# Two PSUM banks as two tiles, splits spread over steps, two activations moved by 128 bytes

## The chip, the cores and the metric

The kernel runs on one core of a Trainium2 chip. The metric is the device time of one execution in microseconds (us); for a kernel that is timed several times it is the median. A profiled execution gives a trace with every instruction; its own time stands beside the span from its first to its last instruction.

## The reference

Packed attention, a multilayer perceptron (MLP) with an ELU-like function, and a second one with a rational function, one after the other on 4608 tokens (8 batches of 576) of 512 features:

```python
p_packed = sm_attn(p, k, v)              # 8 heads x 32 packed rows, softmax over 576 keys
x = sm_attn(q, p_packed, p_packed)       # 576 queries over the 32 packed rows
h = x @ w_in                             # 512 -> 2048
g = np.where(h > 0.0, h, np.exp(np.minimum(h, 0.0)) - 1.0)
x = g @ w_out                            # 2048 -> 512
h = x @ w_in2                            # second MLP, again 512 -> 2048 -> 512
P = a[0] + a[1] * h + a[2] * h2 + a[3] * h3
Q = 1.0 + np.abs(b[0]) * np.abs(h) + np.abs(b[1]) * h2
out = (P / (Q + 1e-06)) @ w_out2
```

The weights of both MLPs come in as float64, read as pairs of 32-bit words. Nearly every product is made of three matmuls: each operand is split in a high part in fp32r (`hi`) and a remainder (`lo`), and hi·hi, hi·lo and lo·hi are added up in PSUM.

## The kernel before

All engine streams are written out by hand in one order; the program waits only where a tile is read or reused. There are two stages.

**Stage one, 256 steps.** A step `s` is one block of 128 hidden units (16 blocks `f`) for one half (`n`, 288 tokens) of one batch (`b`): 32 steps a batch. Its matmuls are six of 288 columns for the hidden block (`a_h`, L387: the stationary tile is `m`, the packed values already multiplied with `w_in`, and the moving tile is `A_all`, the softmax weights) and twelve of 288 columns into four accumulators (`a_o`, L422: stationary `wo`, moving `gl_all`). ACT and DVE work between the two: `a_act1`, `a_dve1` (the activation), `a_hi` (ACT) and `a_lo` (DVE, L412), which make `gl_all`. The loop issues `a_h` of step s+2, the elementwise work of s+1 and s+2, then the queues of this step, then `a_o` of step s.

Everything else of stage one stands in four tables by step: `ldq` (loads), `peq` (further matmuls), `ewq` (elementwise) and `cvq` (weights of the first MLP). They hold the attention of the next batch (`s1h_*`, `t1_*`, `pp_*`, `s2_*`, `m_*`) and two preparations for stage two:
- `x_prep` (L456) takes the 512 finished features of a half batch, forms the four sums of a Winograd product of 2 by 2 blocks, splits each of the seven operands (`up` on ACT, L473, `low` on DVE, L476) and stores both parts to DRAM (`x2d`, L478). Its scratch is reused, so a split can wait for a store.
- `w2_*` does the same with the weights of the second MLP (`s2d` for `w_in2`, `wo2d` for `w_out2`): load, conversion (`w2_up` on ACT, `w2_bits` on DVE, L537 and L541), sums, split, store.

The tile `k` of a batch is loaded by `load_k`, `q` by `load_q1`; both tiles are reused by `x_prep` for its input and scratch. `MS`, `SCH` and the numbers in the loop over `b` set the steps.

**Stage two, 48 windows.** A window `s` (L832) follows the list `PLAN` (L59). It makes the seven block products P1 to P7 (`prod`, L696: six matmuls of 384 columns each) of the pair of hidden blocks s+2, the rational function of pair s+1 on ACT and DVE, and six groups of six output matmuls of 512 columns (`out_mm`, L774) of pair s. The seven products go into two PSUM banks of one tile `ab`: P1, P6, P7, P4 add up in bank 0, and P2, then P5 and P3, use bank 1. Between them the banks are read: `keep` (ACT, L718) copies bank 0 after P1, P6 and P7; `c_add` (DVE, L721) adds bank 1 to such a copy (C11 after P2, C22 after P5, C12 after P3); C21 (ACT, L825) copies bank 0 after P4. On PE the order in a window is P1, o0, P2, o1, P6, o2, P5, P7, o3, o4, P4, o5, P3. In the last steps of stage one (246 to 254) the products of the first two pairs are already issued, by `PUMP` (L1154).

In stage two `A_all` and `gl_all` serve as room for the split activations (`g_tile`, L761).

Of the kernel before, what the change touches and what calls it, by code (L numbers as in the profile page):

```python
# [22 lines left out]
def packed_attention_moe_moe2_kernel(  # L23
# [404 lines left out]
    def a_evac(s):  # L428
# [6 lines left out]
        else:  # L435
            if b == 0 and n == 1:
                x, sc = part[0][:, 1], part[0][:, 0]
            else:
# [2 lines left out]
            sc = [sc[:, i] for i in range(NKD)]
            if b == 0 and n == 0:
                sc += [part[0][:, 0, i] for i in range(NKD)]
            mlp["x", s] = x, sc
# [11 lines left out]
    def x_prep(s):  # L456
# [24 lines left out]
        yield sub(t1, b12, b11), sub(t2, b22, t1), up(P1)  # L481
        yield sub(b12, b22, b12), sub(t4, b21, t2), low(P1)
        if len(sc) > NKD:
            for js in ((P5, P7), (P2, P3), (P6, P4)):
                for j in js:
                    up(j)
                yield
                for j in js:
                    low(j)
        else:  # L490
            for js in ((P5, P7), (P2, P3, P6, P4)):
                yield
                for j in js:
                    up(j)
                yield
                for j in js:
                    low(j)
                yield
# [752 lines left out]
```

## Time and profile before

| | |
|---|---|
| time, median of 3 runs | 1622.56 us (1620.89 to 1624.38) |
| profiled execution | 1621.8 us, its span 1620.0 us |
| PE (matmul) busy | 1511.1 us, 93% |
| PEld (weight load) busy | 1331.3 us, 82% |
| DVE busy | 1248.4 us, 77% |
| ACT busy | 1087.5 us, 67% |
| mean granted clock of TensorE | 0.987 of full speed |
| DMA | 301.13 MB, mean 186 GB/s |

Stage one reaches to about 812 us, stage two from there to the end. A share over the whole span mixes the two stages and the passage between them; the rows below are taken stage by stage. A row of the timeline in square brackets shows how long its engine had been idle before, and what ended that.

### The profile page before, as it was taken

Reading aid. Unit: us, or ns where it says so; the run is one execution under the profiler, and the core shown is the slowest. Engines: PE = TensorE matmul, PEld = TensorE weight load, DVE = VectorE, ACT = ScalarE, POOL = GpSimd, SP = SyncE. Lnnn points to the kernel's source line nnn. Section 1 sums busy time; section 2 is a strip of 40 time slices with the busy share of each in tenths; the row PEclk is TensorE's granted clock in tenths of the full one; section 3 lists DMA queues with packets and bytes.
Section 4 is the critical chain, followed back from the end, with each engine's and each line's share of the span. In section 5 each row is a group of like instructions: output and inputs, shape, how many; then the busy total and the mean of one; then the engine's idle time right before and its main releaser. Section 6 shows DMA issues by size and latency. Waiting matters only on the chain.

```text
span 1620.0 us, 26751 instructions
## 1 busy us (share of the span) xinstructions
PE 1511.1 (93%) x10194; PEld 1331.3 (82%) x10194; DVE 1248.4 (77%) x2078; ACT 1087.5 (67%) x1992; POOL 3.3 (0%) x8
## 2 busy tenths in 40 slices
PE   7898999999999999998699999999999999999997
PEld 5777988898998989797677888888888888888886
DVE  6886776777777776763488888888888888888886
ACT  4865666666766666664477686676777767767665
POOL 0000000000000000000000000000000000000000
PEclk9999999999999999999899999999999999999999
DMA  9524454635555555366357766766667666676541
GB/s 358 169 73 145 135 183 134 182 109 162 150 171 160 173 169 159 120 194 214 120 172 229 257 221 223 245 212 210 217 225 226 231 231 210 232 240 212 179 138 44
DMA packets 184880, 301.13 MB, mean 186 GB/s; under 512 B 13360, under 2 KB 124208, under 8 KB 182960
## 3 DMA queue, kind: packets, MB, share of 16 engines
q1 hardware_dynamic: 184752, 299.42, 57.3%
q8 instruction: 80, 1.31, 0.3%
q14 instruction: 48, 0.39, 0.1%
HBM read 233.84 MB, written 65.54 MB: 185 GB/s over the span
## 4 chain that ended last, share of the span: by engine, by line
PE 66%; DVE 21%; ACT 7%; issue 3%; DMA 2%; SPq 0%; DVEq 0%; ACTq 0%
PE ab L703 20%; PE acc L422 18%; PE acc L778 16%; PE h L387 9%; DVE t L741 5%; DVE t L745 3%; DVE h L721 2%; DVE h_o L721 1%; PE m L343 1%; ACT g L397 1%; ACT g L396 1%; DVE g L402 1%; DVE x L476 1%; ACT gl_all L407 1%; DMA x2d<-x 1%
## 5 line engine op out<-in xcount | busy, mean ns | idle before, releaser
L422 PE MATMUL acc<-gl_all,wo 128*128 128x288 f32 x3072 | 466.5, 300 | 20.3 <-DVE gl_all L412 16.2
L422 PEld LDWEIGHTS acc<-gl_all,wo 128*128 128x128 f32 x3072 | 423.7, 190 | 67.4 <-DVE gl_all L412 21.3
L387 PE MATMUL h<-A_all,m 128*128 128x288 f32 x1536 | 246.5, 296 | 2.0 <-DVE m L357 0.9
L703 PE MATMUL ab<-xs_wi,sw 128*128 128x384 f32 x960 | 202.3, 349 | 33.0 <-DVE h_o L721 12.2
L387 PEld LDWEIGHTS h<-A_all,m 128*128 128x128 f32 x1536 | 218.1, 189 | 3.8 <-DVE m L357 1.6
L703 PEld LDWEIGHTS ab<-xs_wi,sw 128*128 128x128 f32 x960 | 168.4, 191 | 60.8 <-DVE h_o L721 17.3
L407 ACT CAST gl_all<-g 128x288 fp32r<-128x288 f32 x256 | 110.9, 433 | 156.4 <-PE acc L422 93.2
L703 PE MATMUL ab<-xs,sw 128*128 128x384 f32 x912 | 187.0, 344 | 22.5 <-DVE h L721 6.3
L778 PE MATMUL acc<-wo,A_all 128*128 128x512 f32 x768 | 204.6, 393 | 0.0
L412 DVE TENSOR_TENSOR gl_all<-g,gl_all 128x288 fp32r<-128x288 f32 x256 | 116.2, 454 | 111.8 <-ACT gl_all L407 110.8
L703 PEld LDWEIGHTS ab<-xs,sw 128*128 128x128 f32 x912 | 158.2, 188 | 45.4 <-ACT h L825 12.8
L755 DVE SCALAR_TENSOR_TENSOR w<-w,sq 128x768 f32<-128x768 f32 x192 | 182.7, 952 | 5.8
L402 DVE SCALAR_TENSOR_TENSOR g<-g,h 128x288 f32<-128x288 f32 x256 | 115.6, 451 | 86.3 <-ACT g L397 86.1
L778 PEld LDWEIGHTS acc<-wo,A_all 128*128 128x128 f32 x768 | 142.8, 188 | 21.3
L396 ACT ACTIVATE g<-h 128x288 f32<-128x288 f32 x256 | 104.8, 409 | 50.0 <-PE h L387 49.2
L397 ACT ACTIVATE g<-g 128x288 f32<-128x288 f32 x256 | 113.8, 445 | 8.1
L825 ACT COPY h<-ab 128x384 f32<-128x384 f32 x48 | 23.1, 481 | 128.1 <-DVE h L721 128.1
L778 PE MATMUL acc_h<-wo,A_all 128*128 128x512 f32 x384 | 104.2, 393 | 0.0
L759 DVE SCALAR_TENSOR_TENSOR t<-t,cf,w 128x768 f32<-128x768 f32 x96 | 97.6, 1017 | 1.7
L737 DVE SCALAR_TENSOR_TENSOR w<-sq,cf,w 128x768 f32<-128x768 f32 x96 | 97.0, 1011 | 0.2 <-ACT w L727 0.2
L751 ACT ACTIVATE sq<-sq,cf 128x768 f32<-128x768 f32 x96 | 89.7, 935 | 1.6
L748 ACT ACTIVATE sq<-w,cf 128x768 f32<-128x768 f32 x96 | 89.8, 935 | 0.5 <-DVE w L737 0.5
(421 smaller groups left out, 1986.3 us busy)
## 6 DMA issues: line engine op xcount, KB each, us to landing
sw<-s2d SPq DMA_DIRECT2D x144, 512.0 KB, 3.8
wo<-wo2d SPq DMA_DIRECT2D x96, 512.0 KB, 5.0
x2d<-x SPq DMA_DIRECT2D x206, 144.0 KB, 2.1
xs_wi<-x2d SPq DMA_DIRECT2D x20, 768.0 KB, 7.2
xs<-x2d SPq DMA_DIRECT2D x19, 768.0 KB, 7.3
sw<-s2d SPq DMA_DIRECT2D x48, 256.0 KB, 2.8
...
```

The lines of the kernel that those rows point to most:

```text
L387: nc.tensor.matmul(ps[:, :TA], lhsT=m[:, wx, r, c0:c0 + 128], rhs=A[:, ax, r, :], start=(i == 0), stop=(i == 5))
L396: nc.scalar.activation(d["e"], d["h"][:, :TA], AF.Exp)
L397: nc.scalar.activation(d["e"], d["e"], AF.Relu, scale=-1.0, bias=1.0)
L402: nc.vector.scalar_tensor_tensor(d["g"], d["e"], -1.0, d["h"][:, :TA], ALU.mult, ALU.max)
L407: nc.scalar.copy(d["ghi"], d["g"])
L412: nc.vector.tensor_tensor(d["glo"], d["g"], d["ghi"].bitcast(F32), ALU.subtract)
L422: nc.tensor.matmul(acc[m][:, :TA], lhsT=w[:, wx, m * 128:(m + 1) * 128], rhs=d[g], start=(first and i == 0), stop=(last and i == 2))
L703: nc.tensor.matmul(m2["ab"][:, bank, :TU], lhsT=w[:, j % 2, wx, k, :], rhs=x[:, xx, k, :], start=(start and i == 0), stop=(i == 5), skip_g ...
L737: nc.vector.scalar_tensor_tensor(w, m2["sq", f], cf[:, 5:6], w, ALU.mult, ALU.add)
L755: nc.vector.scalar_tensor_tensor(w, w, c, m2["sq", f], ALU.add, ALU.mult)
L759: nc.vector.scalar_tensor_tensor(t, t, cf[:, 0:1], m2["w", f], ALU.add, ALU.mult)
L778: nc.tensor.matmul(acc[i], lhsT=g_tile(p, f, g)[:, i * 128:(i + 1) * 128], rhs=w[:, wx, :], start=(p % NPR == 0 and f == 1 and k == 0), st ...
```

## The change

The loads, sums, splits, products and copies are the same as before in kind; what changes is where they stand, which tile they use, and how a load is cut. Five things are changed.
1. The two PSUM banks of the block products are two tiles (`bank0`, `bank1`), from a pool of their own, instead of two halves of one tile.
2. `x_prep` no longer yields eight pieces that follow step on step; a table `XSTEPS` puts each sum, `up` and `low` on a step. The input of the first half goes into the tile `v`, in the last batch into `k`.
3. The weight preparation of the second MLP follows a table by 32 steps of a batch, in place of starting points 30 steps (`w_in2`) or 5 steps (`w_out2`) apart; the number of splits is the same.
4. `A` and `gl` (stage one) begin 128 bytes further modulo 256 bytes, because a pad of 32 columns stands ahead of `A` and `A` has 64 columns more; the views for stage two skip 32 columns more.
5. `k` of the third batch is loaded at step 26 in place of 30, `v` at 35 (later batches 31) in place of 28, and each `q` in two halves.

```diff
-    SCH = (6, 8, 11, 13, 14), (18, 24), (20, 22, 26, 30)
+    SCH = (6, 8, 11, 13, 14), (18, 22), (20, 23, 26, 30)
...
-    A_all = T2.tile([128, 3, 2, 2, TP], F32R, tag="A", name="A_all")
+    T2.tile([128, 32], F32, tag="pad", name="pad")
+    A_flat = T2.tile([128, 12 * TP + 64], F32R, tag="A", name="A_flat")
+    A_all = A_flat[:, :12 * TP].rearrange("p (a b c x) -> p a b c x", a=3, b=2, c=2)
...
-                t = P.tile([128, 2 * NKD, TA], F32, tag="kq"[n] if n or b in (0, B - 1) else "v", name=f"x2_{s}")
+                t = P.tile([128, 2 * NKD, TA], F32, tag="q" if n else "k" if b == B - 1 else "v", name=f"x2_{s}")
...
+    XSTEPS = (0, "t1 t2 u0", 3, "t3 l0 t4", 4, "u3 u4", 5, "l3", 6, "l4", 8, "u1 u6", 9, "l1 l6 u2 u5", 10, "l2 l5"), (
+        0, "t1 t2 u0", 1, "l0", 2, "t3 t4", 3, "u3 u4", 5, "l3 l4", 6, "u1 u6", 7, "l1 l6 u2 u5", 8, "l2 l5")
...
-                    m2["ab"][:, bank, :TU], lhsT=w[:, j % 2, wx, k, :], rhs=x[:, xx, k, :],
+                    m2["ab"][bank][:, :TU], lhsT=w[:, j % 2, wx, k, :], rhs=x[:, xx, k, :],
...
-        a = A_all.rearrange("p a b c x -> p (a b c x)").rearrange("p (a x) -> p a x", x=2 * TU)
+        a = A_flat[:, 32:32 + 12 * TP].rearrange("p (a x) -> p a x", x=2 * TU)
...
-                at(ldq, o + 28, load_v, b + 2)
-                at(ldq, o + (20 if b else 30), load_k, b + 2)
+                at(ldq, o + (31 if b else 35), load_v, b + 2)
+                at(ldq, o + (20 if b else 26), load_k, b + 2)
...
         for i in range(4):
             c, kt = divmod(i, 2)
-            s = 34 + 30 * i
+            s = NS * (1 + i)
...
-        for f in range(NF):
-            s = 34 + 120 + 5 * f
-            w2_load(s, ("o", f), ("ca", "cb", "cc")[f % 3])
-            w2_split(s + 2, ("o", f), o2_dst(f))
+        slots = [5 * NS + t for t in (10, 14, 21, 28)] + [6 * NS + t for t in (0, 6, 10, 14, 21, 28)] + [
+            7 * NS + t for t in (0, 3, 6, 9, 12, 15)]
+        for i, s in enumerate(slots):
+            f = i // 2 + NPR * (i % 2)
+            d = {6: 3, 14: 3, 21: 6, 28: 3}.get(s % NS, 2) if s < 7 * NS else 2
+            w2_load(s, ("o", f), ("ca", "cb", "cc")[i % 3])
+            w2_split(s + d, s + d - 1, ("o", f), o2_dst(f))
...
-            m2["ab"] = misc("ab")
+            psm[0].close()
+            ps_ab = psm[0].enter_context(
+                tc.tile_pool(name="ps_ab", bufs=1, space=bass.MemoryType.PSUM, reuse_waits="tile"))
+            m2["ab"] = [ps_ab.tile([128, 512], F32, tag=f"bank{i}", name=f"bank{i}") for i in range(2)]
...
-                prep = x_prep(s)
-                for i in range(8):
-                    at(ewq, s + 1 + i, next, prep, None)
+                prep, n = x_prep(s), a_step(s)[1]
+                for i, ops in zip(XSTEPS[n][::2], XSTEPS[n][1::2]):
+                    for op in ops.split():
+                        t = s + (1 if n or s < NS else 4) + i
+                        if op[0] == "t":
+                            at(ewq, t, prep[op])
+                        else:
+                            at(ewq, t, prep["up" if op[0] == "u" else "lo"], int(op[1]))
```

Three places in the programs that are built from the two kernels follow. The first is PE in a window in the middle of stage two, from P2 to P7 (`sw` is the stationary operand of a product, `acc` rows are output matmuls). A wait names the engine or the DMA queue whose counter it looks at. Before:

```order
L703 MATMUL ab<-xs_wi,sw_0_11720 128x384 [waits Activation_49]
L703 MATMUL ab<-xs_wi,sw_0_11720 128x384 x5
L778 MATMUL acc_h_9649<-wo_18_1_11694,A_all 128x512 x3
L778 MATMUL acc_h_9649<-wo_18_0_11692,A_all 128x512 x3
L703 MATMUL ab<-xs_9100,sw_1_11758 128x384 [waits DMAHW6_49,DVE_49]
L703 MATMUL ab<-xs_9100,sw_1_11758 128x384 x5
L778 MATMUL acc_416<-wo_18_1_11694,A_all 128x512 x3
L778 MATMUL acc_416<-wo_18_0_11692,A_all 128x512 x3
L703 MATMUL ab<-xs_9187,sw_1_11758 128x384 [waits Activation_49]
L703 MATMUL ab<-xs_9187,sw_1_11758 128x384 x5
L703 MATMUL ab<-xs_9782,sw_2_11798 128x384 [waits DMAHW3_49]
L703 MATMUL ab<-xs_9782,sw_2_11798 128x384 x5
```

Now:

```order
L690 MATMUL bank_9239<-xs_wi,sw_0_11740 128x384 [waits DVE_49]
L690 MATMUL bank_9239<-xs_wi,sw_0_11740 128x384 x5
L765 MATMUL acc_h_9669<-wo_18_1_11714,A_flat 128x512 x3
L765 MATMUL acc_h_9669<-wo_18_0_11712,A_flat 128x512 x3
L690 MATMUL bank_9238<-xs_9107,sw_1_11778 128x384 [waits DMAHW5_49,Activation_49]
L690 MATMUL bank_9238<-xs_9107,sw_1_11778 128x384 x5
L765 MATMUL acc_421<-wo_18_1_11714,A_flat 128x512 x3
L765 MATMUL acc_421<-wo_18_0_11712,A_flat 128x512 x3
L690 MATMUL bank_9239<-xs_9189,sw_1_11778 128x384 [waits DVE_49]
L690 MATMUL bank_9239<-xs_9189,sw_1_11778 128x384 x5
L690 MATMUL bank_9238<-xs_9802,sw_2_11818 128x384 [waits DMAHW2_49,Activation_49]
L690 MATMUL bank_9238<-xs_9802,sw_2_11818 128x384 x5
```

Each row of six is where it was. P2 (into bank 1) waited for ACT and now waits for DVE; P6 (bank 0) waited for DVE and now waits for ACT; P5 (bank 1) waited for ACT and now for DVE; P7 (bank 0) had no wait for an engine and now has one for ACT.

The second is DVE in step 87 to 88 of stage one, the 24th and 25th step of the third batch (`g` and `gl_all` rows are the step's own work, L476 are `low` of `x_prep`, `w2` the weights). Before:

```order
L310 TENSOR_REDUCE s2m_3_1_3582<-s2x_3_1_3581 128x18
L311 TENSOR_SCALAR s2m_3_1_3582<-s2m_3_1_3582 128x18
L312 RECIPROCAL s2m_3_1_3582<-s2m_3_1_3582 128x18
L357 TENSOR_TENSOR m_3_1_3687<-m_3_1_3669,m_3_1_3687 128x1024
L537 TENSOR_SCALAR w2('i', 0, 3)_cb_3644<-w2('i', 0, 3)_cb_3644 128x512
L541 SCALAR_TENSOR_TENSOR w2('i', 0, 3)_cb_3644<-raw1('i', 0, 3)_3480,w2('i', 0, 3)_cb_3644 128x512
L476 TENSOR_TENSOR x2_79_3410<-x2_79_3410 128x2x144 x2
L476 TENSOR_TENSOR x2_79_3410<-x2_79_3410 128x288 x2
L412 TENSOR_TENSOR gl_all_73<-g_89_3679,gl_all_73 128x288
L402 SCALAR_TENSOR_TENSOR g_90_3724<-g_90_3724,h_90_3716 128x288
L316 TENSOR_TENSOR s2x_3_1_3581<-s2x_3_1_3581,s2m_3_1_3582 128x576
L640 TENSOR_TENSOR w2('s', 1, 4)_cc_3730<-w2('i', 0, 3)_cb_3644,w2('s', 1, 2)_ca_3394 128x512
```

Now, from the same softmax sum on:

```order
L314 TENSOR_REDUCE s2m_3_1_3574<-s2x_3_1_3573 128x18
L315 TENSOR_SCALAR s2m_3_1_3574<-s2m_3_1_3574 128x18
L316 RECIPROCAL s2m_3_1_3574<-s2m_3_1_3574 128x18
L361 TENSOR_TENSOR m_3_1_3677<-m_3_1_3659,m_3_1_3677 128x1024
L416 TENSOR_TENSOR gl_all_77<-g_89_3669,gl_all_77 128x288
L406 SCALAR_TENSOR_TENSOR g_90_3702<-g_90_3702,h_90_3694 128x288
L320 TENSOR_TENSOR s2x_3_1_3573<-s2x_3_1_3573,s2m_3_1_3574 128x576
L476 TENSOR_TENSOR x2_79_3412<-x2_79_3412 128x288
L416 TENSOR_TENSOR gl_all_77<-g_90_3702,gl_all_77 128x288
L406 SCALAR_TENSOR_TENSOR g_91_3731<-g_91_3731,h_91_3723 128x288
L326 STREAM_TRANSPOSE s2y_3_1_3736<-s2x_3_1_3573 128x576
L476 TENSOR_TENSOR x2_79_3412<-x2_79_3412 128x2x144
```

The two weight conversions and three of the four `low` have left the place between two `gl_all` rows; one `low` stands in each of the next two steps.

The third is SP, the queue of all loads and stores, around the load of `k2` (the third batch; `x2d` rows are stores of `x_prep`). Before:

```order
L124 DMA v2_1532<-in_v_dram 128x4x512
L127 DMA v2_1532<-in_v_dram 64x512
L478 DMA x2d_69<-xpart_555 128x2x144
L478 DMA x2d_69<-x2_23_1372 128x2x144
L478 DMA x2d_69<-xpart_555 128x2x144
L478 DMA x2d_69<-x2_23_1372 128x2x144 x5
L112 DMA p2_1602<-in_pT_dram 128x128
L105 DMA k2_1604<-in_kT_dram 128x2304
L513 DMA raw1('i', 2, 0)_1606<-in_w_in2_dram 128x1024
```

Now:

```order
L123 DMA q1_1093<-in_qT_dram 128x4x288 x2
L116 DMA p2_1464<-in_pT_dram 128x128
L109 DMA k2_1466<-in_kT_dram 128x2304
L478 DMA x2d_72<-x2_23_1396 128x2x144 x6
L500 DMA raw1('i', 2, 0)_1694<-in_w_in2_dram 128x1024
L478 DMA x2d_72<-x2_23_1396 128x2x144 x4
L478 DMA x2d_72<-xpart_563 128x2x144 x2
L478 DMA x2d_72<-x2_23_1396 128x2x144 x4
L128 DMA v2_1781<-in_v_dram 128x4x512
L131 DMA v2_1781<-in_v_dram 64x512
```

`p2` and `k2` stand right behind `q1`, ahead of all stores of the first `x_prep`, and `q1` comes in two halves; `v2` stands behind those stores.

## Rows read from the trace of the kernel before

**Rows 1.** Table by stretch: window, us, busy PE, PEld, DVE, ACT, POOL; clock; DMA.

```profile
138.60:694.30 555.70, 532.66 (x4773) 484.51 (x4772) 399.95 (x899) 365.01 (x871) 0.00 (x0) 0.99 0.50 153
423.60:512.40 88.80, 87.40 (x797) 79.92 (x796) 66.05 (x149) 59.83 (x145) 0.00 (x0) 1.00 0.54 160
744.05:812.40 68.35, 48.52 (x259) 45.75 (x259) 24.59 (x42) 28.62 (x55) 0.00 (x0) 0.85 0.54 178
901.10:1577.80 676.70, 645.10 (x3121) 554.00 (x3121) 574.85 (x680) 485.34 (x671) 0.00 (x0) 1.00 0.66 217
1577.80:1620.00 42.20, 33.62 (x144) 27.22 (x142) 29.52 (x35) 22.29 (x30) 0.00 (x0) 0.94 0.17 58
```

**Rows 2.** Waits, 901 to 1578 us: who for whom; us, times, longest.

```profile
ACT h L825 <- DVE h L721: 110.1, 40, 3.2
...
PEld ab L703 <- DVE h_o L721: 24.4, 20, 1.2
...
PEld ab L703 <- ACT h L825: 11.3, 40, 0.6
PEld ab L703 <- ACT s L718: 10.8, 40, 0.3
```

**Rows 3.** Timeline of weight loads in one window: start, us, what, [idle before].

```profile
1153.36 1.07 PEld L703 LDWEIGHTS ab<-xs_wi,sw 128*128 128x128 f32 x6
...
1155.95 0.99 PEld L703 LDWEIGHTS ab<-xs_wi,sw 128*128 128x128 f32 x6 [0.26 <-ACT s L718]
...
1159.44 1.00 PEld L703 LDWEIGHTS ab<-xs,sw 128*128 128x128 f32 x6 [1.23 <-DVE h_o L721]
...
1161.75 2.16 PEld L703 LDWEIGHTS ab<-xs,sw 128*128 128x128 f32 x12
1163.90 2.67 PEld L778 LDWEIGHTS acc<-wo,A_all 128*128 128x128 f32 x12
1166.61 1.12 PEld L703 LDWEIGHTS ab<-xs,sw 128*128 128x128 f32 x6
...
1169.29 0.99 PEld L703 LDWEIGHTS ab<-xg_k,sw 128*128 128x128 f32 x6 [0.28 <-ACT h L825]
1170.27 0.88 PEld L703 LDWEIGHTS ab<-xs_wi,sw 128*128 128x128 f32 x5
```

**Rows 4.** Timeline of DVE in the same window.

```profile
1154.78 0.56 DVE L721 TENSOR_TENSOR h<-u,ab 128x384 f32<-128x384 f32 x1 [0.74 <-PE ab L703]
...
1168.16 0.55 DVE L721 TENSOR_TENSOR h<-s,ab 128x384 f32<-128x384 f32 x1 [1.23 <-PE ab L703]
```

**Rows 5.** Waits of PE, 744 to 812.5 us.

```profile
PE ab L703 <- ACT s L718: 6.7, 4, 2.4
PE ab L703 <- ACT h L825: 4.7, 2, 2.4
PE ab L703 <- DVE h_o L721: 3.4, 1, 3.4
```

**Rows 6.** Timeline of SP and PE at the third batch's `k`.

```profile
140.75 0.35 SPq L105 DMA_DIRECT2D k<-in_kT_dram  x1
...
146.04 1.22 PE L178 MATMUL s1h<-k,p 64*32 64x288 f32 x16 [6.60 <-DMA k<-in_kT_dram]
```

**Rows 7.** Timeline of DVE and ACT in steps 87 to 88.

```profile
308.58 1.56 DVE L476 TENSOR_TENSOR x<-x 128x288 fp32r<-128x288 f32 x4
...
310.95 0.43 ACT L407 CAST gl_all<-g 128x288 fp32r<-128x288 f32 x1 [3.56 <-DVE g L402]
```

**Rows 8.** The page's costliest groups: count, busy us, mean ns, idle before.

```profile
L422 PE MATMUL acc<-gl_all,wo 128*128 128x288 f32 x3072 | 466.5, 300 | 20.3 <-DVE gl_all L412 16.2
...
L387 PE MATMUL h<-A_all,m 128*128 128x288 f32 x1536 | 246.5, 296 | 2.0 <-DVE m L357 0.9
```

**Rows 9.** The chain of waits in order of time: start, us, what.

```profile
740.10 1.58 PE acc L422 x12
...
838.09 2.08 PE ab L703 x12
840.17 2.76 PE acc L778 x12
```

More of the change, by code (lines that the diff above doesn't have):

```diff
@@ L80, in packed_attention_moe_moe2_kernel @@
     ps_w = actx.enter_context(tc.tile_pool(name="ps_w", bufs=1, space=bass.MemoryType.PSUM))
+    psm = [ExitStack()]
+    psm.append(psm[0].enter_context(tc.tile_pool(name="ps_m", bufs=1, space=bass.MemoryType.PSUM)))
     T2 = actx.enter_context(tc.tile_pool(name="T2", bufs=1))
@@ L89, in misc @@
     def misc(name):
-        return ps_w.tile([128, 2, 512], F32, tag="misc", name=name)
-    A_all = T2.tile([128, 3, 2, 2, TP], F32R, tag="A", name="A_all")
+        return psm[1].tile([128, 2, 512], F32, tag="misc", name=name)
+    T2.tile([128, 32], F32, tag="pad", name="pad")
+    A_flat = T2.tile([128, 12 * TP + 64], F32R, tag="A", name="A_flat")
+    A_all = A_flat[:, :12 * TP].rearrange("p (a b c x) -> p a b c x", a=3, b=2, c=2)
     gl_all = T2.tile([128, 4, TP], F32R, tag="gl", name="gl_all")
@@ L438, in a_evac @@
             else:
-                t = P.tile([128, 2 * NKD, TA], F32, tag="kq"[n] if n or b in (0, B - 1) else "v", name=f"x2_{s}")
+                t = P.tile([128, 2 * NKD, TA], F32, tag="q" if n else "k" if b == B - 1 else "v", name=f"x2_{s}")
                 x, sc = t[:, :NKD], t[:, NKD:]
[L441 to L444, printed above, removed]
+            mlp["x", s] = x, [sc[:, i] for i in range(NKD)]
         for m in range(NKD):
@@ L463, in x_prep @@
         src = {P1: b11, P2: b21, P3: b22, P5: t1, P6: t2, P7: b12, P4: t4}
-        tmp = [sc[1]] + sc[4:]
-        hi, free = {}, []
+        tmp, hi = [sc[1]], {}
         u = slice((2 * b + n) * TR, (2 * b + n + 1) * TR)
@@ L479, in low @@
             tmp.extend((hi[j], src[j]))
[L481 to L498, printed above, removed]
+        return dict(t1=lambda: sub(t1, b12, b11), t2=lambda: sub(t2, b22, t1), t3=lambda: sub(b12, b22, b12),
+                    t4=lambda: sub(t4, b21, t2), up=up, lo=low)
+    XSTEPS = (0, "t1 t2 u0", 3, "t3 l0 t4", 4, "u3 u4", 5, "l3", 6, "l4", 8, "u1 u6", 9, "l1 l6 u2 u5", 10, "l2 l5"), (
+        0, "t1 t2 u0", 1, "l0", 2, "t3 t4", 3, "u3 u4", 5, "l3 l4", 6, "u1 u6", 7, "l1 l6 u2 u5", 8, "l2 l5")
     RDT = w_in1.dtype
@@ L717, in keep @@
     def keep(name):
-        nc.scalar.copy(m2[name], m2["ab"][:, 0, :TU])
+        nc.scalar.copy(m2[name], m2["ab"][0][:, :TU])
     def c_add(p, f, half, name):
-        nc.vector.tensor_tensor(h_tiles(p)[f][:, half], m2[name], m2["ab"][:, 1, :TU], ALU.add)
+        nc.vector.tensor_tensor(h_tiles(p)[f][:, half], m2[name], m2["ab"][1][:, :TU], ALU.add)
     def flat(x):
@@ L824, in one @@
         elif name == "C21":
-            nc.scalar.copy(h_tiles(p)[1][:, 0], m2["ab"][:, 0, :TU])
+            nc.scalar.copy(h_tiles(p)[1][:, 0], m2["ab"][0][:, :TU])
         else:
@@ L1011, in load_q1 @@
         def load_q1(b, tag="q"):
-            for _ in load_q(b, tag=tag):
+            for _ in load_q(b, HALVES, tag):
                 pass
@@ L1159, in packed_attention_moe_moe2_kernel @@
                 prox.close()
+                psm[0].close()
                 pacc = actx.enter_context(
@@ L1162, in packed_attention_moe_moe2_kernel @@
                 acc = [pacc.tile([128, 512], F32, tag=f"acc{m}", name=f"acc{m}") for m in range(4)]
+                psm[1] = psm[0].enter_context(
+                    tc.tile_pool(name="ps_m2", bufs=1, space=bass.MemoryType.PSUM, reuse_waits="tile"))
             run(ldq, s)
@@ L1198, in packed_attention_moe_moe2_kernel @@
         t2x.close()
+        psm[0].close()
         actx.close()
```

44 lines of the change are left out of this document (22 added, 22 removed).

## The prediction

> **What bounds the kernel now.** First the table by stretch [rows 1], because the two stages have different limits. In the middle of stage two, 40 windows take 676.70 us, 16.92 us each; PE is busy for 645.10 us of it, and its clock is granted in full (1.00, the 2.4 GHz level). In stage one, six batches of 32 steps with the same work take 555.70 us; the fastest of them takes 88.80 us at 87.40 us of busy PE, so six like it would take 532.8 us. Between the stages lie 68.35 us with 48.52 us of busy PE and a clock of 0.85. So PE bounds both stages, and a gain can come only from its idle time or from the time of one matmul.
>
> Next, what PE waits for. In stage two the waits that end its idle time are all on `ab`, the tile with the two banks of the block products [rows 2]: weight loads wait for DVE's C11 (24.4 us in 20 windows; every second window has another name for the target, so twice that in 40), for ACT's C21 (11.3 us) and for ACT's copy after P1 (10.8 us). The weight loads of one window show where [rows 3]: 0.26 us ahead of P2, 1.23 us ahead of P6, 0.28 us ahead of P3. These waits are not for data. P6 adds to bank 0, and C11, which it waits for, reads bank 1; P2 starts bank 1, and the copy it waits for reads bank 0; P3 adds to bank 1 and waits for C21, which reads bank 0. Behind C11 stand four other DVE instructions since C12, and C12 itself had waited 0.74 us for P1 to end, though it reads what P3 wrote [rows 4]. One tile makes this ring: P1, C12, four instructions of the rational function, C11, P6, and so on to P4, C22, C21, P3, P1.
>
> **The change part by part.** All sums are made against the profiled execution, 1621.8 us (span 1620.0 us and 1.8 us around it); the median of the runs, 1622.56 us, lies 0.8 us higher.
>
> *Two tiles for two banks, stage two.* No instruction is added. The period without these waits is the sum of the distances between groups of weight loads that do not wait [rows 3]. P5 and P7 take 1163.90 - 1161.75 = 2.15 us, 1.075 each; o3 and o4 take 1166.61 - 1163.90 = 2.71 us, 1.355 each. Seven products and six output groups make 7 x 1.075 + 6 x 1.355 = 15.66 us. Against 16.92 that is 1.26 us a window. A bound from the other side is the busy time of PE, 645.10 / 40 = 16.13 us [rows 1], a gain of 0.79; busy time holds the run-out of the matmuls at each of the three stops, so I take the distances. The five windows ahead of these 40 have the same products, so 45 x 1.25 = 56 us (by busy time, 45 x 0.79 = 36).
>
> What is late next? Each product now waits for the reader of its own bank: P2 for C12, P6 for the copy after P1, P5 for C11, P7 for the copy after P6, P4 for that after P7, P3 for C22, P1 for C21. The tightest is P3. DVE was free for C22 at 1168.16 - 1.23 = 1166.93 [rows 4]; it waited there for P4, which writes the other bank. Without that it ends at 1166.93 + 0.55 = 1167.48, while PE comes to P3 only at 1166.61 + 1.11 + 1.355 = 1169.08: 1.6 us to spare. C21, which waited for C22 (110.1 us in 40 windows, on ACT), follows P4 at once, and P1 comes two groups after. Then the load of the two engines: DVE works 574.85 / 40 = 14.37 us a window and ACT 485.34 / 40 = 12.13 [rows 1]. Both are below 15.66, DVE by 1.29 us, and of its present idle time the 0.74 ahead of C12 and the 1.23 ahead of C22 are waits that go or shrink. So I let PE keep the bound, with little room on DVE.
>
> *The passage.* Fourteen products are issued there between steps of stage one. Each copy or addition stands behind the step's own work on ACT and DVE, and the next product waits for it. The three largest groups are 6.7 + 4.7 + 3.4 = 14.8 us of idle PE [rows 5]. With two tiles each wait falls on the product after, which has a step's matmuls (12 x 0.132 = 1.58 us of output, 0.79 of hidden block) or another product (1.05 us) before it; waits up to some 2 us vanish, longer ones shrink. The later split of the last batch's first half (steps 243 to 253 in place of 240 to 247) puts more of its fourteen splits beside these waits, at 0.4 us each by the four `low` of 1.56 us [rows 7]. The bounds are 0 and the whole loss, 68.35 less the work (some 38 us by matmul durations), 30. I take 14.
>
> *Splits spread, `k` sooner.* `k` of the third batch is issued at 140.75 us and PE idles 6.60 us for it [rows 6]; around it the queue holds stores of `x_prep`, whose scratch was in the same tile. It is now issued four steps earlier and the scratch lies elsewhere, so the wait goes. Step 88 shows the other loss: two conversions and four `low` (1.56 us) stand together ahead of `a_lo`, and ACT then idles 3.56 us, since the next activation comes late [rows 7]. Now no step has more than two or three such additions, at an equal number of instructions. If all six batches ran like the fastest, 555.70 - 532.8 = 22.9 us would go [rows 1]. Not all stops have to vanish, but the fastest batch has 1.4 us of idle PE of its own too; I take 23, with bounds 7 (only `k`) and 30. The first batch, bound by the first MLP's weights, I leave at nothing. The halves of `q` cost seven more issues on SP, under loads that land before they are read; if one came late it would cost a microsecond per batch, 7 us in all.
>
> *The end.* In the last 42.20 us the products of the last pair go through the same ring with a clock of 0.94; I take 2 us.
>
> *A and gl moved by 128 bytes.* This touches 3072 + 1536 = 4608 matmuls [rows 8], all of 288 columns. Twelve take 1.58 us, 131.7 ns each [rows 9]; 288 columns at 2.4 GHz are 120.0 ns, so 11.7 ns lie on top. Twelve of 384 columns take 2.08 us, 13.3 ns over 160.0; twelve of 512 take 2.76 us, 16.7 over 213.3. No row shows another address of the moving tile in this stage, so I bound it by the whole excess, 4608 x 11.7 = 54 us, and as much on the other side. The nearest rows are the wider matmuls, whose tiles begin on other offsets and whose excess differs by 2 to 5 ns without regard to sense; the value I take is 0.
>
> The Trainium skill (TensorE: Matmul & The Clock Gate, section "Back-to-back issue gap") gives about N / 2.4 + 2.5 ns for a warm matmul, 122.5 ns for 288 columns; here the rows differ, 131.7 ns. The same page ("Step-by-step: what each phase is for") says that weights and moving operand have read ports of their own, by which an address would cost nothing; no run here shows that yet. If the 9.2 ns between page and rows came from where the tiles lie, 4608 x 9.2 = 42 us could go.
>
> The sum: 56 + 14 + 23 + 2 = 95 us, 1621.8 - 95 = 1526.8 us; on the scale of the median 1527.6, rounded to 1528.
>
> **The rivals.**
> *The address counts.* The excess of 11.7 ns falls by 9 or so, since the moving tile then no longer meets the weight load in the same part of the memory. For it: an excess of that size stands on every matmul, whatever its width. Against it: nothing in the rows ties it to an address. It gives some 42 us more: 1486 us.
> *Another wait takes over in stage two.* DVE has 1.29 us of room, and its order is fixed: the last `lo` waits for ACT's `hi`, which stands behind C21 and so behind P4. If half of the room turns out to be wait, the period is 16.3 us: 45 x 0.6 = 27 in place of 56, 1557 us. For it speaks DVE's 85% in [rows 1]; against it, that its waits of today are nearly all for `ab`.
> *The banks are still guarded together.* Then only the spreading counts, 23 + 2: 1598 us. The waits of the built program speak against it.
> *The address counts the wrong way, slower than before.* Price: to eat 95 us, 95 / 4608 = 20.6 ns on each narrow matmul of stage one, that is, from 152 ns on. With the excess tripled (155 ns) the time is 1528 + 108 = 1636 us. Against it: no group of rows has an excess above 17 ns.
>
> **How the numbers follow.** Forecast 0.60, address 0.20, another wait 0.15, banks together 0.03, slower 0.02. The likeliest case has its own range from 1508 (the passage and stage one at their upper bounds) to 1545 (stage two by busy time). The range of 8 in 10 takes in the middle of the address case and the other wait: 1482 to 1562. About 0.2% is what a measurement here can tell from no change. All cases but the last end well below; 0.02 more I keep for what is in none of them, half of it on either side of no change: faster 0.96, same 0.01, slower 0.03.
>
> **What would show it.** In the profile after: P1 to P1 in stage two at 15.7 us and no wait of PE on a bank; C12 and C22 without a wait for PE behind them, and DVE at 92% there (14.37 / 15.66). Stage one: batches near 88 us and no wait for `k`; twelve matmuls of 288 columns still at 1.58 us, or at 1.46 if the address counts. The passage near 54 us. The prediction is wrong if the period of a window stays above 16.2 us with PE waiting, or if the time of twelve matmuls moves.

## The result and the profile after

The changed kernel takes 1539.08 us (median of 4 runs, 1537.46 to 1540.97) against 1621.78 us (median of 4 runs, the three of the first table and one more): a ratio of 0.9488, interval 0.9472 to 0.9505, 82.7 us less. Forecast were 1528 us and 95 us less. The profiled execution, the longest of the four, took 1540.97 us with a span of 1539.2.

The table by stretch after (columns as in [rows 1]): batches 1 to 6; steps 224 to 245 of batch 7; the passage; windows 0 to 4; windows 5 to 44; the end.

```profile
136.98:678.39 541.41, 528.07 (x4772) 478.68 (x4772) 394.31 (x892) 365.06 (x866) 0.00 (x0) 1.00 0.49 150
678.39:736.38 57.99, 53.79 (x399) 52.02 (x398) 35.33 (x80) 36.51 (x89) 0.00 (x0) 1.00 0.72 230
736.38:791.00 54.62, 42.94 (x260) 41.09 (x260) 26.78 (x48) 29.33 (x57) 0.00 (x0) 0.94 0.69 235
791.00:873.00 82.00, 79.63 (x392) 69.94 (x391) 76.31 (x99) 61.47 (x88) 0.00 (x0) 1.00 0.70 224
873.00:1498.60 625.60, 625.60 (x3122) 563.00 (x3121) 574.70 (x681) 485.11 (x672) 0.00 (x0) 1.00 0.71 235
1498.60:1539.20 40.60, 31.51 (x144) 25.84 (x142) 28.11 (x34) 21.68 (x30) 0.00 (x0) 0.96 0.19 58
```

The table below puts every profiled execution on these stretches; they are cut where PE ends the last product of a step, or the first output product of a window. All columns are in us; the labels are those of the experiments, and the last column is the median of a kernel's runs (one run for e10 and e11).

| kernel | to the end of batch 0 | batches 1-6 | 7, to step 245 | passage | windows 0-4 | 5-44 | end | median |
|---|---|---|---|---|---|---|---|---|
| before | 135.8 | 556.1 | 52.1 | 68.6 | 88.7 | 676.7 | 42.0 | 1621.8 |
| after | 137.0 | 541.4 | 58.0 | 54.6 | 82.0 | 625.6 | 40.6 | 1539.1 |
| e1 tiles alone | 135.8 | 554.3 | 52.3 | 53.4 | 78.9 | 625.6 | 40.2 | 1542.4 |
| e2 address alone | 135.5 | 554.6 | 51.7 | 68.4 | 88.7 | 677.1 | 41.5 | 1619.3 |
| e3 one tile again | 136.6 | 540.2 | 56.6 | 68.1 | 91.3 | 676.6 | 42.9 | 1615.4 |
| e4 old address | 138.8 | 542.8 | 57.9 | 54.6 | 82.2 | 625.6 | 40.4 | 1542.6 |
| e5 tiles, k sooner | 137.1 | 545.5 | 52.9 | 53.3 | 78.9 | 625.6 | 39.9 | 1534.9 |
| e6 q apart | 136.5 | 530.6 | 55.6 | 53.1 | 81.6 | 625.6 | 39.7 | 1525.5 |
| e7 scratch in pairs | 137.0 | 539.2 | 57.0 | 56.0 | 81.8 | 625.6 | 40.7 | 1534.5 |
| e9 x's splits | 136.5 | 540.8 | 54.6 | 55.9 | 79.3 | 625.6 | 40.9 | 1533.8 |
| e8 all mended | 136.4 | 529.1 | 51.5 | 54.6 | 79.3 | 625.6 | 40.5 | 1517.9 |
| e12 mended again | 136.4 | 524.8 | 51.5 | 56.2 | 79.3 | 625.6 | 39.8 | 1513.5 |
| e10 `gl` alone moved | 136.8 | 544.0 | 58.3 | 56.1 | 81.7 | 625.6 | 41.3 | 1545.6 |
| e11 both by 64 bytes | 136.8 | 544.0 | 60.6 | 51.6 | 81.8 | 626.0 | 40.6 | 1543.2 |

Before to after: -1.2 in the beginning, 14.7 in batches 1 to 6, -5.9 in batch 7, 14.0 in the passage, 6.7 and 51.1 in the windows, 1.4 at the end; together 80.8, the difference of the two spans. Single executions vary: up to step 245 (the first three columns) e3 and the changed kernel do the same and differ by 3.0 us.

*Stage two.* The waits from 873 to 1498.6 us (waiter, releaser: us, times, longest), against [rows 2]. PE is not among the waiters: it is busy for all 625.60 us.

```profile
ACT h L812 <- PE bank L690: 71.2, 40, 1.9
ACT s L705 <- PE bank L690: 40.3, 40, 1.2
...
DVE h_o L708 <- PE bank L690: 4.6, 20, 0.2
DVE h L708 <- PE bank L690: 4.6, 20, 0.2
```

What is left on DVE is C12's wait of 0.2 us for P3, whose sum it reads. One window of weight loads, and the two additions of DVE in it, against [rows 3, 4]:

```profile
1139.65 1.12 PEld L690 LDWEIGHTS bank<-xs_wi,sw 128*128 128x128 f32 x6
...
1142.08 1.12 PEld L690 LDWEIGHTS bank<-xs_wi,sw 128*128 128x128 f32 x6
...
1144.52 2.16 PEld L690 LDWEIGHTS bank<-xs_wi,sw 128*128 128x128 f32 x12
...
1151.82 2.16 PEld L690 LDWEIGHTS bank<-xs,sw 128*128 128x128 f32 x12
```

```profile
1149.96 0.55 DVE L708 TENSOR_TENSOR h<-s,bank 128x384 f32<-128x384 f32 x1
...
1153.29 0.56 DVE L708 TENSOR_TENSOR h_o<-u,bank 128x384 f32<-128x384 f32 x1 [0.23 <-PE bank L690]
```

No load has idle time ahead of it. C22 starts at 1149.96 without a wait and ends at 1150.51; P3 follows at 1151.82, 1.3 us later (forecast 1.6). Each of the 40 windows takes 15.64 us.

*The passage.* PE still waits for the banks there: all its own waits for them (rows `PE`; the rows `PEld` are the weight loads at the same stops) come to 11.7 us, against 19.7 before, of which [rows 5] shows 14.8. These waits are nearly all of PE's idle time in this stretch. The rest of the 14.0 us is busy time of PE, 42.9 us in place of 48.8. The granted clock, between its levels of 1.2 and 2.4 GHz, rose there from 0.85 to 0.94 of full.

```profile
PEld bank L690 <- DVE h L708: 4.9, 2, 2.7
...
PE bank L690 <- DVE h L708: 4.4, 2, 2.5
...
PEld bank L690 <- DVE h_o L708: 3.4, 2, 2.2
PEld bank L690 <- ACT s L705: 3.1, 2, 1.6
```

*`k`.* SP's queue issues it 53 us sooner than in [rows 6], and PE has no wait for it:

```profile
87.33 0.66 SPq L109 DMA_DIRECT2D k<-in_kT_dram  x1
```

*The address.* Two groups of the page against [rows 8], and twelve matmuls on the chain against [rows 9] (1.58 us there):

```profile
L426 PE MATMUL acc<-gl_all,wo 128*128 128x288 f32 x3072 | 462.3, 298 | 23.4 <-ACT gl_all L411 12.5
...
L391 PE MATMUL h<-A_flat,m 128*128 128x288 f32 x1536 | 243.7, 294 | 2.1 <-DVE m L361 0.9
```

```profile
644.27 1.56 PE acc L426 x12
```

The mean distance between the ends of neighbouring matmuls of 288 columns (those under 150 ns, some 4400) went from 131.4 to 130.2 ns; a bare step of 18 of them from 2.37 to 2.34 us.

*New stops in stage one.* The old ones ([rows 6, 7] and some smaller) are gone, but a step that should take 2.34 us now takes 3.2 to 3.6 at the fifth step of batches 1 to 6, 3.1 to 4.0 at steps 47, 48, 80, 111, 112, 143, 144, 168 and 176, 5.51 at 232, 3.3 to 3.4 at 206, 236, 239 and 240; and step 205, 3.19 without a stop (e7), takes 6.99, 3.55 before. All the others took 2.37 before, except 69 (3.55), 80 (2.63) and 165 (2.90). Three kinds of wait make them. The first, at step 205 (waits, 625 to 629.8 us; then SP's queue ahead of it; then the transfers' sizes and their us from issue to landing):

```profile
ACT whi('o', 3)_7862 L632 <- DMA wo2d<-whi('o', 10)_7719: 6.3, 1, 6.3
PEld acc L426 <- ACT gl_all L411: 3.3, 1, 3.3
```

```profile
615.98 1.23 SPq L123 DMA_DIRECT2D q<-in_qT_dram  x2
617.25 0.62 SPq L500 DMA_DIRECT2D raw1('o', 11)_7742<-in_w_out_dram  x1
617.91 0.46 SPq L639 DMA_DIRECT2D wo2d<-whi('o', 10)_7719  x1
```

```profile
q<-in_qT_dram SPq DMA_DIRECT2D x2, 576.0 KB, 5.1
...
wo2d<-whi('o', 10)_7719 SPq DMA_DIRECT2D x1, 256.0 KB, 7.8
...
wo2d<-whi('o', 3)_7862 SPq DMA_DIRECT2D x1, 256.0 KB, 2.0
```

ACT cannot write the next high part into the scratch `whi` until the store of the last one has landed. That store takes 2.0 us by itself, but 7.8 behind q's 1152 KB and a raw weight of 512 KB. It was also issued late: the high part was ready at 611.15 us and its store was issued at 617.91, since the stores of `x` and the load of q stand ahead of it in SP's order. That load waits in turn for those stores, because q's tile is the scratch of `x` (SP's waits, 600 to 626 us):

```profile
SPq L123 <- DMA x2d<-x: 1.8, 2, 1.4
```

So 14.6 us lie between the end of the high part and the landing of its store, 6.8 of them ahead of the issue. The Trainium skill (DMA: Bandwidth & Descriptors, section "Queues, rings and completion order") says that each DMA engine takes the descriptors of a queue in the order of its ring; the landings here agree: q's halves at 620.3 and 622.4 us, the raw weight at 625.1, the store at 625.7. Step 47 is the same with another scratch: ACT waits 4.6 us for a store of `cb` behind q. At steps 48, 80, 112 and 144, the first of a half batch, PE waits until ACT (L450, 0.7 us) and DVE (L452) have copied the accumulators of the half batch before; ACT comes to that late behind the same wait for `cb`, and at step 176 behind one of 3.7 us for a raw weight. The second kind is the sum of ACT's own work, at step 165 (timeline of ACT):

```profile
508.97 0.62 ACT L632 CAST whi('i', 1, 3)_6397<-w2('i', 1, 3)_cb 128x512 fp32r<-128x512 f32 x1
509.48 0.77 ACT L473 CAST x<-x 128x288 fp32r<-128x288 f32 x2
510.15 0.43 ACT L411 CAST gl_all<-g 128x288 fp32r<-128x288 f32 x1
```

Behind the softmax of the next batch stand a high part of a weight and the two of x (u3, u4), and only then the `a_hi` for which PE waits. The third is x's scratch against x's own stores: at step 168 (ACT waits 2.8 us), at step 232 (first line; waits, 697 to 702.8 us), and in window 3, where two steps' work is issued together (the others; waits, 838.4 to 857.2 us):

```profile
ACT x L473 <- DMA x2d<-x: 4.2, 1, 4.2
...
ACT x L473 <- DMA x2d<-x: 3.4, 1, 3.4
...
PEld bank L690 <- ACT s L705: 1.7, 1, 1.7
```

### The profile page after: what moved, and what is told of

It is laid out like the page before. It is cut to its first block, busy times and chain, and to the rows that moved or that the text cites. A ratio compares the mean times of both kernels' runs of the same rounds, so it can differ in the third digit from the quotient of the medians.

```text
span 1539.2 us, 26771 instructions
## 1 busy us (share of the span) xinstructions
PE 1479.9 (96%) x10194; PEld 1329.7 (86%) x10194; DVE 1246.3 (81%) x2078; ACT 1088.9 (71%) x1992; POOL 3.3 (0%) x8
## 4 chain that ended last, share of the span: by engine, by line
PE 74%; DVE 11%; ACT 7%; DMA 5%; issue 2%; SPq 0%; POOL 0%; ACTq 0%; DVEq 0%; POOLq 0%
PE bank L690 22%; PE acc L426 16%; PE acc L765 16%; PE acc_h L765 8%; PE h L391 8%; PE m L347 2%; DVE g L406 1%; ACT g L401 1%; ACT g L400 1%; DMA x2d<-x 1%; ACT E L206 1%; ACT gl_all L411 1%; DVE gl_all L416 1%; DVE w L742 1%; PE pp L248 1%
## 5 line engine op out<-in xcount | busy, mean ns | idle before, releaser
L391 PE MATMUL h<-A_flat,m 128*128 128x288 f32 x1536 | 243.7, 294 | 2.1 <-DVE m L361 0.9
L391 PEld LDWEIGHTS h<-A_flat,m 128*128 128x128 f32 x1536 | 215.4, 188 | 3.9 <-DVE m L361 1.6
L765 PE MATMUL acc<-wo,A_flat 128*128 128x512 f32 x768 | 204.2, 393 | 0.0
L690 PE MATMUL bank<-xs_wi,sw 128*128 128x384 f32 x960 | 192.1, 337 | 6.7 <-DVE h_o L708 2.8
L690 PE MATMUL bank<-xs,sw 128*128 128x384 f32 x912 | 181.0, 337 | 9.6 <-DVE h L708 6.3
L690 PEld LDWEIGHTS bank<-xs_wi,sw 128*128 128x128 f32 x960 | 170.9, 189 | 18.4 <-DVE h_o L708 3.4
L690 PEld LDWEIGHTS bank<-xs,sw 128*128 128x128 f32 x912 | 162.0, 188 | 20.0 <-DVE h L708 7.5
L765 PEld LDWEIGHTS acc<-wo,A_flat 128*128 128x128 f32 x768 | 142.5, 188 | 21.3
L765 PE MATMUL acc_h<-wo,A_flat 128*128 128x512 f32 x384 | 104.3, 393 | 0.0
L756 ACT CAST A_flat<-t 128x768 fp32r<-128x768 f32 x72 | 60.3, 837 | 38.2 <-DVE t L746 38.2
```

The lines of the kernel that those rows point to most:

```text
L391: nc.tensor.matmul(ps[:, :TA], lhsT=m[:, wx, r, c0:c0 + 128], rhs=A[:, ax, r, :], start=(i == 0), stop=(i == 5))
L690: nc.tensor.matmul(m2["ab"][bank][:, :TU], lhsT=w[:, j % 2, wx, k, :], rhs=x[:, xx, k, :], start=(start and i == 0), stop=(i == 5), skip_g ...
L765: nc.tensor.matmul(acc[i], lhsT=g_tile(p, f, g)[:, i * 128:(i + 1) * 128], rhs=w[:, wx, :], start=(p % NPR == 0 and f == 1 and k == 0), st ...
```

## The experiments

**e1, the two tiles alone**, in the kernel before: the lines of the change on `psm`, `ps_ab` and `m2["ab"]`.

> The kernel before with the two PSUM banks as two tiles and nothing else. Theory A (the gain of each part stands by itself, as the trace after was read): stage two gains its whole 59 us (windows at 15.64 us against 16.91) and the passage its 14, so about 1549 us; stage one keeps its old stops. Theory B (the passage's gain comes from the later splits of the last batch's first half): the 59 us alone, about 1563 us with the passage still near 68 us.

Measured: 1542.39 us (ratio 0.9516, 0.9503 to 0.9529). The passage and windows 5 to 44 in its table by stretch:

```profile
742.40:795.80 53.40, 41.86 (x260) 39.80 (x260) 24.90 (x43) 28.85 (x55) 0.00 (x0) 0.97 0.67 224
874.70:1500.30 625.60, 625.60 (x3121) 563.01 (x3121) 574.70 (x681) 485.38 (x672) 0.00 (x0) 1.00 0.71 235
```

The passage did not stay at 68 us, so it is A; the time lies 7 us below A's 1549. The tiles by themselves bring 79.2 us, where the whole change brings 82.7, and more in windows 0 to 4 (9.7) than they do in the changed kernel (6.7), which has the stop in window 3. The change gives them a pool of their own; e3 keeps that pool and joins the tiles.

**e2, the address alone**, in the kernel before (the tile `g3` of stage two is moved as well, as in the change).

```
+    T2.tile([128, 32], F32, tag="pad", name="pad")
+    A_flat = T2.tile([128, 12 * TP + 64], F32R, tag="A", name="A_flat")
...
```

> The kernel before with A, gl and g3 moved as in the change and nothing else. Theory A (the address takes 1.7 ns off each of the 4608 matmuls of 288 columns): the bare step of stage one goes from 2.37 to 2.34 us, the pitch from 131.7 to 130.0 ns, and the time to about 1614 us. Theory B (the shorter step comes from the new spreading of work on the other engines): pitch still 131.7 ns and 1622 us.

Measured: 1619.26 us (0.9986, 0.9976 to 0.9996), 2.3 us less; distance 130.2 ns, bare step 2.34 us. So it is the address and not the spreading that shortens the matmul, as A says, though by 1.2 ns and not by A's 1.7. Of 4608 x 1.2 ns = 5.5 us less than half arrives, and the time lies nearer to B's 1622 us than to A's 1614.

**e3, one tile again**, in the changed kernel.

```
-            m2["ab"] = [ps_ab.tile([128, 512], F32, tag=f"bank{i}", name=f"bank{i}") for i in range(2)]
+            ab = ps_ab.tile([128, 2, 512], F32, tag="ab", name="ab")
+            m2["ab"] = [ab[:, i] for i in range(2)]
```

> The changed kernel with both banks in one tile again. Theory A (parts add up): it loses 59 us in stage two and 14 in the passage, 1539 + 73 = 1612 us. Theory B (passage owes its gain to the splits): 1539 + 59 = 1598 us.

Measured: 1615.39 us (0.9967, 0.9956 to 0.9977), as A (1612): 76.3 us are lost again with the pool in place, so the two tiles bring them. The passage is back at 68.1 us, at a clock of 0.85, although the later splits are in it. All that spreading, `k` and address bring without the tiles is 6.2 us (before: 1621.60 on that chip).

**e4, the old address** in the changed kernel: the lines of e2 taken out.

> The changed kernel with A, gl and g3 back at their old addresses. Theory A (address): pitch back at 131.7 ns, 1539 + 8 = 1547 us, so the spreading of the splits by itself is worth next to nothing. Theory B (spreading): pitch stays at 130.0 ns and 1539 us.

Measured: 1542.58 us, 3.5 above the changed kernel; distance 131.3 ns. A's direction, less than half its size (8 us).

**e5, `k` sooner**, on top of e1.

```
-                t = P.tile(..., tag="kq"[n] if n or b in (0, B - 1) else "v", ...)
+                t = P.tile(..., tag="q" if n else "k" if b == B - 1 else "v", ...)
-                at(ldq, o + 28, load_v, b + 2)
-                at(ldq, o + (20 if b else 30), load_k, b + 2)
+                at(ldq, o + (31 if b else 35), load_v, b + 2)
+                at(ldq, o + (20 if b else 26), load_k, b + 2)
```

> The kernel before with the two tiles (as in e1) and with k and v of the third batch loaded at the change's places, the first batch's x in v's tile; all splits at their old steps. Theory A (what the spreading brought is the wait for k alone): batch 1 falls from 99.8 to about 90.5 us and the time from 1542.4 to about 1533, below the whole change. Theory B (batch 1 needs the new splits too): batch 1 stays above 95 us and the time above 1538.

Measured: 1534.92 us (0.9456, 0.943 to 0.9483). Batch 1, by stretch:

```profile
137.11:227.61 90.50, 87.50 (x797) 79.94 (x797) 67.05 (x152) 60.17 (x143) 0.00 (x0) 1.00 0.49 150
```

99.8 us became 90.5, as A says: 7.0 us of it are idle time of PE, and 2.3 busy time, as the clock granted in this batch goes from 0.95 to 1.00. Two tiles and `k` without any spreading are 4.2 us faster than the whole change, which has the address besides. Against e4, which has tiles, `k` and spreading but the old address, the spreading (with the halves of q) costs 7.7 us. (e1 and e4 were timed on another chip than e5; the kernel before differs by 0.5 us between the two.)

**e6, q's halves apart**, in the changed kernel.

```
-                at(ldq, o + NS + 9, load_q1, b + 2)
+                lq2 = load_q(b + 2, HALVES)
+                at(ldq, o + NS + 9, next, lq2)
+                at(ldq, o + NS + 15, next, lq2)
```

> The changed kernel with the second half of q issued six steps after the first, in place of directly behind it. Theory A (the new stops of steps 47, 48, 80, 111, 112, 143, 144 and 205 come from stores of the split weights that stand on SP's queue behind q's 1152 KB, and so free their scratch late): they shrink or go, 14.6 us of idle PE at most, about 1528 us. Theory B (ACT is simply overloaded in these steps): the stops stay, 1539 us.

Measured: 1525.53 us (0.9402, 0.9383 to 0.9421), 13.6 less than the change. SP's queue at the place of step 205, and the wait there (600 to 640 us):

```profile
609.02 0.56 SPq L123 DMA_DIRECT2D q<-in_qT_dram  x1
...
610.28 0.43 SPq L639 DMA_DIRECT2D wo2d<-whi('o', 10)_7719  x1
```

```profile
ACT whi('o', 3)_7861 L632 <- DMA wo2d<-whi('o', 10)_7719: 3.5, 1, 3.5
```

ACT's wait is 3.5 us in place of 6.3 and hardly reaches PE (step 205: 3.62 us). The store now lands 5.6 us after its issue in place of 7.8; the delay ahead of its issue, 6.2 us, is nearly what it was. Steps 47, 48, 111, 143 and 176 are bare; 112 and 144 keep 0.3 to 0.5 us. Step 80 keeps its whole stop, against A: its store of `cb` lands 6.1 us after its issue, 6.3 in the changed kernel, although only half of q stands ahead of it. So A holds for most of the stops, and what holds that store stays open.

**e7, scratch in pairs**: the output weights' value and high part go to (`ca`, `cb`) and (`cc`, `whi`) in turn, in place of three tiles for values and `whi` for every high part.

> The changed kernel with the four scratch tiles of the second MLP's output weights used in two pairs (value and its high part), in place of three for the values and one for all the high parts. Theory A (the stops of steps 205, 236, 239 and 240, 8 us together, are waits of ACT for the store of the high part before, out of the one tile for high parts): these go, about 1532 us; step 232, which waits for a store of x, stays at 5.5 us. Theory B (the DMA queue is too full in these places whatever the scratch): the waits move to the tiles of the values and the time stays within 2 us of 1539.

Measured: 1534.47 us (0.9461, 0.9436 to 0.9486), 4.6 less than the change, where A has about 7. Step 205 takes 3.19 us and 236 and 239 are bare, as A says; but step 240 now takes 4.35 us. From 690 to 728 us:

```profile
ACT x L473 <- DMA x2d<-x: 4.3, 1, 4.3
ACT w2('o', 7)_ca L518 <- DMA wo2d<-w2('o', 6)_ca: 3.1, 1, 3.1
```

In batch 7 the wait has moved to the tile of a value, as B says; why those stores are late is not shown. Step 79, which this edit does not touch, took 4.71 us in this execution and 2.34 in the changed kernel: ACT waited there 5.3 us for the store of `cb` in place of 2.9. So a single execution's stops vary by a few us.

**e9, x's splits anew**: u3 and u4 one step later; for the last two batches wider distances.

```
-        0, "t1 t2 u0", 1, "l0", 2, "t3 t4", 3, "u3 u4", 5, "l3 l4", 6, "u1 u6", 7, "l1 l6 u2 u5", 8, "l2 l5")
+        0, "t1 t2 u0", 1, "l0", 2, "t3 t4", 4, "u3 u4", 5, "l3 l4", 6, "u1 u6", 7, "l1 l6 u2 u5", 8, "l2 l5"), (
+        0, "t1 t2 u0", 1, "l0", 2, "t3 t4", 4, "u3 u4", 5, "l3 l4", 9, "u1 u6", 10, "l1 l6", 11, "u2 u5", 12, "l2 l5"), (
+        0, "t1 t2 u0 l0", 1, "t3 t4", 2, "u3 u4", 3, "l3 l4", 5, "u1 u6 u2 u5", 7, "l1 l6 l2 l5")
...
```

> The changed kernel with only x's second halves placed anew: u3 and u4 one step later, the last two batches' splits further apart. Theory A (the stop at the fifth step of each of the batches 1 to 6 is the sum of ACT's work in the step where u3 and u4 stand, 1.07 us each; the stop in window 3 and that at step 232 wait for stores of x): 6.4 + 3.1 + 3.2 us less, about 1526. Theory B (the fifth step is held by DVE or by the softmax): the six stops stay, about 1533 us.

Measured: 1533.8 us (0.9455, 0.9437 to 0.9473). The two stops that A puts down to stores of x are gone, window 3 taking 15.66 us and step 232 taking 2.34, but the time is that of B (1533), not A's 1526. ACT at step 165:

```profile
507.67 0.62 ACT L634 CAST whi('i', 1, 3)_6397<-w2('i', 1, 3)_cb 128x512 fp32r<-128x512 f32 x1
508.18 0.44 ACT L411 CAST gl_all<-g 128x288 fp32r<-128x288 f32 x1
```

`a_hi` follows the weight's high part at once, and the fifth steps lose some 0.6 of the 1.07 us that A gives each (in batch 6 only 0.2); up to 0.4 stays. Part of the gain is lost again: step 205 grew to 8.4 us, 47 to 4.8, 236 to 4.2.

**e8, all mended**: e6, e7 and e9 together, the fourth weight piece of a batch three steps later, `x_load` three steps later, and

```
-        slots = [5 * NS + t for t in (10, 14, 21, 28)] + [6 * NS + t for t in (0, 6, 10, 14, 21, 28)] + [
-            7 * NS + t for t in (0, 3, 6, 9, 12, 15)]
+        slots = [5 * NS + t for t in (10, 14, 17, 21, 27)] + [6 * NS + t for t in (0, 3, 6, 9, 12, 15, 21, 27)] + [
+            7 * NS + t for t in (0, 3, 6)]
...
```

> The changed kernel with e6 and e7 together, u3 and u4 of x's second half one step later (ACT has 3.2 us of work in the step they stood in), the first batches' fourth weight piece three steps later, the output weights' pieces at 13 places of batches 5 and 6 and 3 of batch 7 in place of 10 and 6, x_load three steps later, and the last batch's splits in the windows two apart. Theory A (the 23 us of the forecast were there, and new waits on stores took them): stage one's batches 1 to 6 near 87 us each, batch 7 near 52.5, no stop in window 3, about 1513 us. Theory B (stage one is held by something else, as by the sum of work on ACT and DVE): above 1530.

Measured: 1517.91 us (0.9354, 0.9334 to 0.9374), A's 1513 but for a new stop at steps 205 and 206 (4.5 us together), where ACT waits 6.0 us for a store (`wo2d` out of `cc`) that again stood behind q, here its first half.

**e12, mended again**: the two pieces of batch 6 at 12 and 15 go to 14 and 17.

> As e8, with the pieces of batch 6 that stood at steps 12 and 15 at 14 and 17, away from q's load. Theory A (in e8 the stop of 4.4 us at step 205 is ACT waiting for a store that stood behind q on SP's queue): the stop goes, about 1513 us. Theory B (it moves to the next piece): 1518 us.

Measured: 1513.46 us (0.9331, 0.9316 to 0.9345), as A: step 205 takes 3.56 us. Batches 1 to 6 and batch 7 by stretch:

```profile
136.42:661.21 524.79, 522.00 (x4773) 476.57 (x4772) 400.17 (x902) 368.37 (x872) 0.00 (x0) 1.00 0.52 162
661.21:712.69 51.48, 51.48 (x398) 51.48 (x398) 30.40 (x70) 34.53 (x83) 0.00 (x0) 1.00 0.60 186
```

This version beats both kernels: 108.9 us under the one before, 25.6 under the changed one. PE idles 2.8 us in six batches.

**e10, `gl` alone at the new address**, and **e11, both moved by 64 bytes** (one run each).

> The changed kernel with A at its old address and gl alone at its new one. Theory A (each moving tile's own address sets the pitch of its matmuls): between two matmuls that read gl 130.2 ns, between two that read A 131.2. Theory B (the pitch belongs to the whole pattern): both alike.

> The changed kernel with A and gl moved by 64 bytes in place of 128 (stage two's tiles stay where they are). Theory A (what counts is whether the moving tile lies as the weights do, in steps of 64 bytes or less): 130.2 ns as with 128. Theory B (it takes 128 bytes): 131.3 ns as without a move.

Measured: in e10 130.4 ns between matmuls that read `gl` and 131.9 between those that read `A` (before 131.4 and 131.2, after 130.2 and 130.1): each tile's own address counts, as A says, though A's theory gives 131.2 for `A` and not 131.9. In e11 131.1 and 130.8: neither theory, about a third of the way. The times, 1545.6 and 1543.2 us, are single runs.

## Why the prediction was right, and where a term was not

*Two tiles in stage two, 56 us.* Right: 51.1 + 6.7 = 57.8 us, and 60.8 with the tiles alone (e1). The period of 15.64 us is the sum of distances (15.66); busy time, the bound of 36, was too low, as PE's busy time after is the whole of its 625.60 us. No wait of PE on a bank is left in windows 5 to 44, P3 has 1.3 us to spare (1.6 forecast), DVE is at 574.70 / 625.60 = 92%. The rivals "another wait takes over" and "still guarded together" fall.

*The passage, 14 us.* The size came, 14.0, but not as it was made up, and that is luck. The forecast took all of it from PE's waits. These gave 8.0 us; the other 6 are busy time of PE, for which the forecast had no term. Most of that goes with the clock. All kernels with two tiles have 11.5 to 11.7 us of idle PE there, and their PE is busy for 39.9 us at a granted clock of 1.00 (e11), 41.4 to 41.8 at 0.97 (e1, e5, e6), 42.9 at 0.94 (the changed kernel, e4, e8) and 44.2 to 44.5 at 0.91 (e7, e9, e10, e12). With one tile (before, e2, e3) it is busy for 48.6 to 49.1 us at 0.85, with 19.0 to 19.9 idle. So the stretch differs by 4.6 us, 51.6 to 56.2, between kernels that wait alike. The gain comes from the tiles, which alone give 15.2 (e1). The splits that the forecast set beside the waits bring next to nothing: with one tile they give 0.5 (e3), and at one clock, 0.97, the stretch takes 53.4 and 53.3 us without the later splits (e1, e5) and 53.1 with them (e6).

*Stage one, 23 us.* This is the step that failed. The forecast took the fastest batch as the measure for six, because "no step has more than two or three such additions, at an equal number of instructions". That counts DVE's work. Measured are 14.7 us in the six batches, less 5.9 in batch 7 and 1.2 in the beginning: 7.7. By the time at which step 245 ends, `k` brings 6.9 of them (e1 to e5) and the address 3.0 (e4 to the changed kernel), the spreading with q's halves costs 3.9 (e5 to e4), and 1.7 lie between the kernel before and e1, where nothing of stage one was moved; single executions can differ by 3 us here. In the whole time `k` brings 7.5 us and the spreading costs 7.7, of which some 3 are the stop in window 3. Against the shortest time that each step takes in any of the kernels that were timed several times and have its address, the stops of the six batches were 33.8 us before and are 22.7 now; the shorter bare steps give the other 3.6 of the 14.7. So the old stops went nearly whole, and new ones came in their place.

What was missed are the three kinds of new wait, and two of them are DMA: a conversion that was moved next to the last one that used its scratch has to wait for that one's store, and the store waits on SP's queue behind q. The forecast priced q at 7 us if a half came late. It came late twice, 1.1 us in all (0.4 before); the larger price, with no term, were the stores held up behind it: 13.6 us went when the second half was issued later (e6). ACT's sum in a step was not taken at all (e9). And batch 7, where six of the sixteen pieces of output weights now stand beside `x_load`, had no term. The 23 us were there to be had: e12, which keeps the spreading and mends most of these waits, runs the six batches in 524.8 us, 31 less than before, of which the address has at most 4 (six batches of 576 matmuls, 3456 x 1.2 ns).

*The end, 2 us; the first batch, 0.* 1.4 and -1.2; the first changes by as much between kernels alike in it.

*The address, 0 with bounds of 54 each way.* Nearly right; the forecast's "still at 1.58 us" became 1.56: 1.2 ns of 131.4, worth 2.3 (e2) or 3.5 us (e4). So the time of twelve matmuls did move, which the forecast had named as a sign of being wrong, but by 1%, and the rival with 42 us falls. The Trainium skill (TensorE: Matmul & The Clock Gate, section "Step-by-step: what each phase is for") gives weights and moving operand read ports of their own, so that the address should cost nothing; the runs differ by that 1.2 ns. The same page ("Back-to-back issue gap") has N / 2.4 + 2.5 ns for a warm matmul taken by itself, an estimate of 122.5 ns for 288 columns; the best mean distance in any run here is 130.1.

So the sum was 14 us too hopeful against the profiled spans (95 for 80.8): 15.3 in stage one, with the address's few us counted there, and 0.6 at the end, less 1.8 in stage two. Of the signs that the forecast named, the window of 15.64 us, DVE at 92%, `k` without a wait and the passage came; the batches took 88.6 to 92.2 us and not 88. What stays open: why a tile's address changes the matmul by a nanosecond, why less than the whole of it reaches the time, what holds the store ahead of step 80 in e6, and the 0.4 us that remain at the fifth steps.
